# Batch 1's first half computed second, and the attention of the first two chunks in plain float32 with two heads side by side on the array

## The chip, the cores and the metric

The kernel runs on one core of a Trainium2 chip. The metric is the device time of one execution in microseconds. Names of engines in the profile: PE is TensorE's matmuls, PEld its weight loads, DVE is VectorE, ACT is ScalarE, POOL is GpSimd, SP is the queue from which all DMAs are issued.

## What is computed

Attention with a few sink positions and a sliding window, and behind it a two-layer MLP with a squared ReLU. Batch 4, 8 heads, 768 positions, head dimension 64; `n_sink` is 4 and `window` 128 at run time; the MLP has width 512 and inner width 2048.

```python
scores = (1 / sqrt(64)) * q @ k.T
keep = (k_pos < n_sink) | ((0 <= q_pos - k_pos) & (q_pos - k_pos < window))
a = exp(where(keep, scores, -1e9) - max); a = a / (a.sum(-1) + 1e-9)
x = (a @ v) as (batch * seq, heads * 64)
h = x @ w_in; out = (s * relu(h)**2 + b) @ w_out
```

## The kernel before

The work is cut into eight chunks of 384 positions, a half of a batch each, in the order of batches and halves. A chunk is attended by eight heads in blocks of 128 queries, and then goes through the MoE function (`moe_steps`, L513): for each of 16 tiles of the inner width, `l1` (L524: 12 matmuls of 384 columns, then ReLU, square, and a split into a high and a low part) and, two tiles later, `l2` (L543: 9 matmuls of 512 columns). While chunk c is in its MoE, the attention of chunk c+1 is interleaved with it, slot by slot (L691 to L703).

Products are made with two numbers each in a fast format, a rounded high part and the remainder (tiles of type float32r), except in the first chunk. For chunks 1 to 7 (`attn_slots`, L389) q, k, v and the turned probabilities are split so (L268 to L279, L321, L322), scores are two matmuls of up to 272 columns (L293, L294), and sums of the sink positions and the reciprocals go through a matrix of their own (L305 to L386). A second half has four key blocks, a first half three. Chunk 0 (`first_slots`, L419) has nothing to hide behind and is computed in plain float32: q is held twice, with zeros for the other head of its pair (L429, L430), and for each head and block there is one score product over all 128 partitions (L446), mask and maximum (L448), exponential (L452), after a head's three blocks the scaling by its reciprocal sum (L460 to L463), transposes (L471) with a copy (L475), and the product with v of both heads, of which one half of the partitions is kept (L483 to L486).

The 16 weight tiles come as raw 64-bit words and are made into float32 pairs during chunk 0's attention and MoE (`make_weight`, L189): two conversions on ScalarE (L198, L199), two bit operations on VectorE (L200, L201), an addition on GpSimd (L203), a rounding copy on ScalarE (L208) and the remainder (L214), on GpSimd for one tile in four, else on VectorE. Raw words wait in the place of the next tile; those of the last tile lie in two `g` buffers (L178), of which `l1` has three.

The program is written in slots and steps, but a planner puts each engine's queue in an order by the readiness that it computes, and gives out buffers; only marked instructions keep the program's order.

## Time and profile before

| | us |
|---|---|
| median of three runs (lowest, highest) | 776.92 (775.92, 777.3) |
| the profiled execution | 775.58 |
| its span, first to last instruction | 773.6 |
| TensorE busy (matmuls) | 733.7, 95% |
| VectorE busy | 514.3, 66% |
| ScalarE busy | 501.5, 65% |
| GpSimd busy | 269.6, 35% |

The busy shares are means over stretches that differ. A stretch is read in the table of windows, an instruction's price in the groups by line, an order and a wait in the timelines. A matmul's end is modelled, so the distance between starts tells more than a duration.

### The profile page before, as it was taken

The page shows a single profiled execution, that of the slowest core. Times are in us where ns is not written, and L with a number is a line of the kernel's source. Part 1 is how long each engine was busy: PE and PEld are TensorE (multiplying, and loading weights), DVE is VectorE, ACT ScalarE, POOL GpSimd, SP SyncE. Part 2 cuts the span into 40 slices and gives each one's busy share as a digit, 9 for nine tenths or more (in the row PEclk, how much of TensorE's full clock was granted, in tenths as well). Part 3 has the DMA queues.
Part 4 walks back from the last instruction along what each step waited for, and adds up shares of the span by engine and source line. Part 5 has one row for each costly group of instructions (what it writes and reads, how often), then busy time and mean ns, then how long its engine had stood idle before and what let it go on. Part 6 is the DMA issues. An engine that isn't in the chain of part 4 may idle for free.

```text
span 773.6 us, 12079 instructions
## 1 busy us (share of the span) xinstructions
PE 733.7 (95%) x3980; PEld 652.9 (84%) x3980; DVE 514.3 (66%) x1251; ACT 501.5 (65%) x1231; POOL 269.6 (35%) x439
## 2 busy tenths in 40 slices
PE   6888887799999999999999999999999999999996
PEld 3567675589989999999989999999999999899985
DVE  5988998985676566765676566765676566763221
ACT  3996977776676577666676576766676576653222
POOL 3147567652333234332334234332334234310000
PEclk8998998889999999999999999999999999999999
DMA  8644304212111211112111211112112211001001
GB/s 271 277 146 182 112 14 162 86 34 76 44 44 53 86 47 54 50 44 77 43 44 55 85 47 54 50 43 77 43 43 57 84 47 54 29 1 42 0 1 46
DMA packets 28117, 54.21 MB, mean 70 GB/s; under 512 B 3600, under 2 KB 16528, under 8 KB 26128
## 3 DMA queue, kind: packets, MB, share of 16 engines
q1 hardware_dynamic: 28048, 53.36, 21.4%
q8 instruction: 34, 0.56, 0.3%
q14 instruction: 35, 0.29, 0.1%
HBM read 47.06 MB, written 6.29 MB: 69 GB/s over the span
## 4 chain that ended last, share of the span: by engine, by line
PE 76%; DVE 8%; ACT 7%; POOL 3%; issue 2%; DMA 1%; SPq 1%; POOLq 0%; ACTq 0%; DVEq 0%
PE h L524 32%; PE po L543 29%; PE o L355 3%; PE sc L294 2%; PE sc L293 2%; PE tp L317 2%; POOL w L203 2%; PE tp L316 2%; DVE w L201 1%; DVE g L532 1%; ACT w L199 1%; PE os L381 1%; DMA sb<-in_s 1%; PE ts L370 1%; DVE wt L200 1%
## 5 line engine op out<-in xcount | busy, mean ns | idle before, releaser
L543 PE MATMUL po<-w,g 128*128 128x512 f32 x1152 | 304.2, 404 | 7.6 <-ACT g L531 4.2
L524 PE MATMUL h<-x,w 128*128 128x384 f32 x1536 | 302.6, 346 | 6.3 <-DVE r L529 1.9
L524 PEld LDWEIGHTS h<-x,w 128*128 128x128 f32 x1536 | 272.5, 192 | 13.2 <-DVE r L529 3.2
L543 PEld LDWEIGHTS po<-w,g 128*128 128x128 f32 x1152 | 210.2, 190 | 49.6 <-DVE g L532 5.6
L527 ACT ACTIVATE r<-h 128x384 f32<-128x384 f32 x128 | 62.8, 491 | 104.2 <-PE h L524 97.6
L298 DVE CUSTOM_DVE_ANT_0 sm<-sc,msk 128x272 f32<-128x272 f32 (+1 forms) x168 | 70.0, 417 | 73.6 <-PE sc L294 64.4
L532 DVE SCALAR_TENSOR_TENSOR g<-r,sb,g 128x384 fp32r<-128x384 f32 x128 | 88.0, 687 | 45.6 <-ACT g L531 43.5
L529 DVE SCALAR_TENSOR_TENSOR r<-h,sb,r 128x384 f32<-128x384 f32 x128 | 78.5, 613 | 50.7 <-ACT r L527 50.6
L305 POOL COPY psk<-sm 128x48 f32<-128x48 f32 x168 | 47.0, 280 | 166.4 <-ACT sm L304 165.7
L304 ACT ACTIVATE sm<-sm,negm 128x272 f32<-128x272 f32 (+1 forms) x168 | 85.2, 507 | 23.4 <-DVE negm L298 17.4
L531 ACT ACTIVATE g<-r,sb 128x384 fp32r<-128x384 f32 x128 | 78.7, 615 | 27.7 <-DVE r L529 25.9
L273 POOL TENSOR_TENSOR kl<-kraw,kh 128x544 fp32r<-128x544 f32 (+1 forms) x56 | 71.5, 1277 | 54.9 <-ACT kh L271 50.8
L321 ACT CAST hl<-tp 128x256 fp32r<-128x256 f32 (+1 forms) x168 | 59.0, 352 | 24.1 <-PE tp L317 23.6
L322 DVE TENSOR_TENSOR hl<-tp,hl 128x256 fp32r<-128x256 f32 (+1 forms) x168 | 66.6, 397 | 6.2 <-ACT hl L321 5.3
L278 POOL TENSOR_TENSOR vv<-vraw,vv 128x256 fp32r<-128x256 f32 (+1 forms) x56 | 40.8, 728 | 54.1 <-ACT vv L277 49.7
L364 DVE TENSOR_TENSOR xm<-o,y 64x512 f32<-64x512 f32 x56 | 38.5, 687 | 31.3 <-ACT y L363 18.9
L355 PE MATMUL o<-hl,vv 128*128 128x256 f32 (+1 forms) x288 | 54.5, 288 | 0.8 <-DVE r L529 0.7
L294 PE MATMUL sc<-kl,qs 128*128 128x272 f32 (+1 forms) x168 | 48.8, 291 | 0.3 <-POOL kl L273 0.3
L293 PE MATMUL sc<-kh,qs 128*128 128x272 f32 (+1 forms) x168 | 47.6, 283 | 1.4 <-DVE hl L322 1.4
L203 POOL TENSOR_TENSOR w<-w 128x1024 int32<-128x1024 int32 (+1 forms) x17 | 32.9, 1934 | 37.4 <-DVE z L461 19.4
L317 PE MATMUL tp<-identr,sm 128*128 128x128 f32 x168 | 45.9, 273 | 0.0
L272 DVE TENSOR_TENSOR qs<-qraw,qs 64x384 fp32r<-64x384 f32 x56 | 40.4, 721 | 6.9 <-ACT qs L268 5.3
(116 smaller groups left out, 895.5 us busy)
## 6 DMA issues: line engine op xcount, KB each, us to landing
w<-in_w SPq DMA_DIRECT2D x15, 1024.0 KB, 10.0
kraw<-in_kT SPq DMA_DIRECT2D x32, 272.0 KB, 2.6
out<-ot SPq DMA_DIRECT2D x24, 256.0 KB, 2.0
qraw<-in_qT SPq DMA_DIRECT2D x28, 192.0 KB, 2.4
kraw<-in_kT SPq DMA_DIRECT2D x24, 208.0 KB, 2.4
vraw<-in_v SPq DMA_DIRECT2D x16, 256.0 KB, 2.7
vraw<-in_v SPq DMA_DIRECT2D x12, 192.0 KB, 2.3
vsraw<-in_vsk SPq DMA_DIRECT2D x28, 64.0 KB, 1.8
```

The source lines that it names most:

```text
L273: nc.gpsimd.tensor_tensor(out=hd.kl[:, :kw], in0=hd.k[:, :kw], in1=hd.kh[:, :kw].bitcast(F32), op=ALU.subtract)
L293: nc.tensor.matmul(sc[:, :n], hd.qs[:, qs], hd.kh[:, c0:c0 + n], start=True, stop=False)
L294: nc.tensor.matmul(sc[:, :n], hd.qs[:, qs], hd.kl[:, c0:c0 + n], start=False, stop=True)
L298: nc.vector.tensor_tensor_reduce(out=sm[:, :n], in0=sc[:, :n], in1=m, scale=-0.125, scalar=BIG, op0=ALU.add, op1=ALU.min, accum_out=negm[: ...
L304: nc.scalar.activation(sm[:, :n], sm[:, :n], AF.Exp, bias=negm[:, uu], scale=-1.0, accum_out=pp.zz[:, i, hh:hh + 1])
L322: nc.vector.tensor_tensor(out=lo, in0=tp[:, a:z], in1=hi.bitcast(F32), op=ALU.subtract)
L355: nc.tensor.matmul(hd.o[:, q0:q0 + n * P], hd.vv[:, kb, :], hd.hl[:, t, c0 * P:(c0 + n) * P], start=(hd.n == 0), stop=(i == BLK - 1 and kb ...
L524: nc.tensor.matmul(h[:, :CH], weight[f][:, 0, wi, cc * P:(cc + 1) * P], x[xi][:, cc, :], start=(i == 0), stop=(i == 11))
L529: nc.vector.scalar_tensor_tensor(out=r, in0=h[:, :CH], scalar=sw_ap, in1=r, op0=ALU.mult, op1=ALU.mult)
L531: nc.scalar.activation(gg[:, 0, :], r, AF.Identity, bias=b_ap, scale=1.0)
L532: nc.vector.scalar_tensor_tensor(out=gg[:, 1, :], in0=r, scalar=b_ap, in1=gg[:, 0, :].bitcast(F32), op0=ALU.add, op1=ALU.subtract)
L543: nc.tensor.matmul(po[tb], gg[:, gi, tsl], weight[f][:, 1, wi, :], start=(f == 0 and i == 0), stop=(f == NF - 1 and i == 2))
```

## The change

The chunks run in the order (batch, half) = (0,0), (1,0), (0,1), (1,1), (2,0), (2,1), (3,0), (3,1). The first two are computed by a new class `Plain` in float32, without the split into parts; both are first halves. The two heads of a pair are worked on together: the score product of each reads its 64 partitions of q and k, the product with v writes its 64 partitions of one PSUM bank, the transposes of both heads fill a bank, and one copy on ScalarE takes 512 columns. VectorE scales, ScalarE copies. Chunk 1's plain attention stands beside chunk 0's MoE, uses tiles of the split form for its own, and loads q, k and v of a pair into one buffer each. q is loaded once and without zeros. The loads of `s` and `b` go out behind the first pair's q and k, and `sw_ap` (L685) keeps its program order. The remainder of the weights is made on GpSimd for every second tile. The raw words of the last tile lie in four pieces, in `vv`, `vv`, `xm` and `y`. The weights' making starts one slot pair earlier. The diff, without the body of `first_slots`, which goes:

```diff
--- before.py
+++ after.py
@@ -15,6 +15,7 @@
 
 P = 128
 B, H, S, D = 4, 8, 768, 64
+ORDER = ((0, 0), (1, 0), (0, 1), (1, 1), (2, 0), (2, 1), (3, 0), (3, 1))
 NS = 16
 BLK = 3
 CH = BLK * P
@@ -31,7 +32,8 @@
 WARM0 = 14
 NARROW, NEARLY = 2, 8
 RB, VB = 2, 2
-E0, LB0, LC0 = 8, 4, 6
+E0 = 8
+FN, FB, FC = (4, 2), (6, 6), (9, 10)
 LB, LC, LD, L2 = 2, 4, 1, 2
 
 
@@ -52,7 +54,7 @@
     first_cm = tc.tile_pool(name="first", bufs=1)
     first = first_cm.__enter__()
     late = []
-    m_all = first.tile([P, 6 * P], MDT, tag="m", name="m_all")
+    m_all = const.tile([P, 6 * P], MDT, tag="m", name="m_all")
     m_full = [m_all[:, a * P:(a + j + 1) * P] for j, a in ((0, 0), (1, 1), (2, 3))]
 
     identr = const.tile([P, P], F32R, tag="identr", name="identr")
@@ -90,7 +92,7 @@
     nc.sync.dma_start(lim[:, 0, :], n_sink.partition_broadcast(P))
     nc.sync.dma_start(lim[:, 1, :], window.partition_broadcast(P))
 
-    sc0 = wk.tile([P, 8, P], F32, tag="g", name="sc0", bufs=3)
+    sc0 = first.tile([P, 8, P], F32, tag="sc0", name="sc0")
     rel, rel1, low, upp, kix, snk, tmp, tm2 = (sc0[:, j, :] for j in range(8))
 
 
@@ -108,7 +110,7 @@
 
         limf = const.tile([P, 4], F32, tag="limf", name="limf")
         tc.keep_in_program_order(nc.vector.tensor_copy(limf[:, 0:2], lim[:, :, 0].bitcast(U32)))
-        nc.vector.tensor_copy(limf[:, 2:4], lim[:, :, 1])
+        tc.keep_in_program_order(nc.vector.tensor_copy(limf[:, 2:4], lim[:, :, 1]))
         nc.vector.scalar_tensor_tensor(out=nw, in0=limf[:, 2:4], scalar=4294967296.0, in1=limf[:, 0:2],
                                        op0=ALU.mult, op1=ALU.add)
         nc.vector.tensor_scalar(out=nw, in0=nw, scalar1=0.0, scalar2=1024.0, op0=ALU.max, op1=ALU.min)
@@ -174,9 +176,9 @@
                 raws[f] = [raw.rearrange("p c (f t) -> p c f t", t=2)]
         else:
             raws[f] = []
-            for c in range(2):
-                raw = wk.tile([P, DM, 2], I32, tag="g", name="wraw", bufs=3)
-                nc.sync.dma_start(raw.rearrange("p f t -> p (f t)"), w[f, :, c, :])
+            for j, tag in enumerate(("vv", "vv", "xm", "y")):
+                raw = wk.tile([P, DM // 2, 2], I32, tag=tag, name="wraw", bufs=2 if tag == "vv" else 1)
+                nc.sync.dma_start(raw.rearrange("p f t -> p (f t)"), w[f, :, j // 2, j % 2 * DM:(j % 2 + 1) * DM])
                 raws[f].append(raw)
 
     def scratch(f, j):
@@ -184,7 +186,15 @@
         if len(raws[f]) == 1:
             tag = f"w{NF - 2 + f % 2}"
             return (late[0] if late else first).tile([P, 2, DM], I32, tag=tag, name="wt", bufs=1)
-        return wk.tile([P, DM], I32, tag="ot", name="wt")
+        return wk.tile([P, DM], I32, tag="ot", name="wt")[:, :raws[f][j].shape[1]]
+
+    def piece(f, j, t):
+
+        n = len(raws[f])
+        if n == 1:
+            return weight[f][:, :, t, :]
+        a = DM * 2 // n
+        return weight[f][:, j * 2 // n, t, j * a % DM:j * a % DM + a]
 
     def make_weight(j):
 
@@ -204,14 +214,12 @@
         if j % 2 == 1:
             weight[f] = place(f).bitcast(F32R)
             for c, raw in enumerate(raws[f]):
-                d = weight[f][:, :, 0, :] if len(raws[f]) == 1 else weight[f][:, c, 0, :]
-                nc.scalar.copy(d, raw[..., 1].bitcast(F32))
+                nc.scalar.copy(piece(f, c, 0), raw[..., 1].bitcast(F32))
         f -= 1
         if j % 2 == 0 and f >= 0:
             for c, raw in enumerate(raws[f]):
-                d = weight[f] if len(raws[f]) == 1 else weight[f][:, c]
-                e = nc.gpsimd if f % 4 == 3 else nc.vector
-                e.tensor_tensor(out=d[..., 1, :], in0=raw[..., 1].bitcast(F32), in1=d[..., 0, :].bitcast(F32), op=ALU.subtract)
+                e = nc.gpsimd if f % 2 == 1 else nc.vector
+                e.tensor_tensor(out=piece(f, c, 1), in0=raw[..., 1].bitcast(F32), in1=piece(f, c, 0).bitcast(F32), op=ALU.subtract)
             raws.pop(f)
 
 
@@ -220,7 +228,7 @@
 
     def new_chunk(c):
         k = Chunk()
-        k.c, k.b, k.half = c, c // 2, c % 2
+        k.c, (k.b, k.half) = c, ORDER[c]
         k.x = [wk.tile([P, NCC, CH], F32R, tag=f"x{i}", name=f"x{i}_{c}") for i in range(2)]
         k.cc, k.xx, k.heads, k.pairs = {}, {}, {}, {}
         return k
@@ -416,98 +424,139 @@
         return k, [slot(t) for t in range(n + LC + LD)]
 
 
-    def first_slots():
...
+    class Plain:
+
+        def __init__(self, c):
+            self.c, (self.b, _) = c, ORDER[c]
+            self.groups = ((0, 1), (2,))
+            if c == 0:
+                self.q = wk.tile([P, NCC, CH], F32, tag="x0", name="q0")
+                self.k = wk.tile([P, NCC, CH], F32, tag="x1", name="k0")
+                self.v = first.tile([P, NCC, BLK, 2, D], F32, tag="v0", name="v0")
+            self.x = [wk.tile([P, NCC, CH], F32R, tag=f"x{i}", name=f"x{i}_{c}") for i in range(2)]
+            self.pairs = {}
+
+        def load_first(self, ps_):
+            nc.sync.dma_start(self.q[:, ps_, :], qT[0, ps_, :, :CH].rearrange("r e s -> e r s"))
+            nc.sync.dma_start(self.k[:, ps_, :], k0[0, :, ps_, :])
+
+        def load_values(self):
             for ps_ in (slice(0, 1), slice(1, NCC)):
+                nc.sync.dma_start(self.v[:, ps_].rearrange("p r n h d -> p r n (h d)"),
+                                  v[0, ps_, :, :BLK].rearrange("r p n h d -> p r n (h d)"))
+
+        def load(self, pr):
+            pp = Chunk()
+            self.pairs[pr] = pp
+            if self.c == 0:
+                pp.q, pp.k, pp.v = self.q[:, pr], self.k[:, pr], self.v[:, pr]
+                return
+            pp.q = wk.tile([P, CH], F32, tag="qraw", name="qf", bufs=1)
+            nc.sync.dma_start(pp.q, qT[self.b, pr, :, :CH])
+            pp.k = wk.tile([P, CH], F32, tag="kraw", name="kf", bufs=1)
+            nc.sync.dma_start(pp.k, k0[1, :, pr, :])
+            pp.v = wk.tile([P, BLK, 2, D], F32, tag="vraw", name="vf", bufs=1)
+            nc.sync.dma_start(pp.v, v[self.b, pr, :, :BLK])
+
+        def scores(self, pr, group):
+
+            pp = self.pairs[pr]
+            if group == 0:
+                pp.sm = [None] * 4
+                pp.z = (wk if self.c else first).tile([P, 2, BLK, 2], F32, tag="zr" if self.c else "z0", name="zf", bufs=2)
+            banks = {}
+            for i in self.groups[group]:
                 for hh in range(2):
                     hs = slice(hh * D, (hh + 1) * D)
...
+                    j = (i // 2, hh)
+                    if j not in banks:
+                        banks[j] = ps("sc")
+                    c0, n = (0, P, 0)[i], (i + 1) * P
+                    nc.tensor.matmul(banks[j][:, c0:c0 + n], pp.q[hs, i * P:(i + 1) * P], pp.k[hs, :n], start=True, stop=True)
+            for i in self.groups[group]:
+                c0, n = (0, P, 0)[i], (i + 1) * P
+                for hh in range(2):
+                    j = 2 * (i // 2) + hh
+                    if pp.sm[j] is None:
+                        if self.c:
+                            tag = ("kh", "kl", "qs")[self.turn % 3]
+                            self.turn += 1
+                            pp.sm[j] = wk.tile([P, CH], F32, tag=tag, name="smf")
+                        else:
+                            pp.sm[j] = first.tile([P, CH], F32, tag="sm0", name="sm0", bufs=E0)
+                    sm = pp.sm[j][:, c0:c0 + n]
+                    u = (self.c * H + 2 * pr + hh) * BLK + i
+                    uu = slice(u, u + 1)
+                    nc.vector.tensor_tensor_reduce(out=sm, in0=banks[(i // 2, hh)][:, c0:c0 + n], in1=m_full[i], scale=-0.125, scalar=BIG,
+                                                   op0=ALU.add, op1=ALU.min, accum_out=negm[:, uu])
+                    nc.scalar.activation(sm, sm, AF.Exp, bias=negm[:, uu], scale=-1.0, accum_out=pp.z[:, 0, i, hh:hh + 1])
+
+        def norm(self, pr):
+
+            pp = self.pairs[pr]
+            nc.vector.tensor_scalar(out=pp.z[:, 1], in0=pp.z[:, 0], scalar1=1e-9, scalar2=None, op0=ALU.add)
+            nc.vector.reciprocal(out=pp.z[:, 0], in_=pp.z[:, 1])
+            for i in range(BLK):
+                c0, n = (0, P, 0)[i], (i + 1) * P
+                for hh in range(2):
+                    sm = pp.sm[2 * (i // 2) + hh][:, c0:c0 + n]
+                    nc.vector.tensor_scalar(out=sm, in0=sm, scalar1=pp.z[:, 0, i, hh:hh + 1], scalar2=None, op0=ALU.mult)
+
+        def turned(self, pr, part):
+
+            pp = self.pairs[pr]
+            if part == 0:
+                pp.t = (wk if self.c else first).tile([P, 2, 2 * BLK, P], F32, tag="hl" if self.c else "tt0", name="tf", bufs=2)
+            tp = (ps if self.c else po_bank)("tp")
+            pos = (((0, 0), (2, 2)), ((1, 0), (1, 1)), ((2, 0), (2, 1)))[part]
+            for hh in range(2):
+                for j, (i, kb) in enumerate(pos):
+                    c0 = (0, P, 0)[i] + kb * P
+                    nc.tensor.transpose(tp[:, (2 * hh + j) * P:(2 * hh + j + 1) * P], pp.sm[2 * (i // 2) + hh][:, c0:c0 + P], ident)
+            out = pp.t[:, :, part:part + (6 if part == 0 else 3):(5 if part == 0 else 2)]
+            nc.scalar.copy(out, tp.rearrange("p (h k c) -> p h k c", h=2, c=P))
+
+        def values(self, pr):
+            pp = self.pairs.pop(pr)
+            o = ps("o")
             for kb in range(BLK):
...
+                for hh in range(2):
+                    a = (0, 3, 5)[kb]
+                    hs = slice(hh * D, (hh + 1) * D)
+                    nc.tensor.matmul(o[hs, kb * P:CH], pp.v[:, kb, hh], pp.t[:, hh, a:a + BLK - kb].rearrange("p k c -> p (k c)"),
+                                     start=(kb == 0), stop=(kb == BLK - 1))
+            nc.scalar.copy(self.x[0][:, pr, :], o[:, :CH])
+            nc.vector.tensor_tensor(out=self.x[1][:, pr, :], in0=o[:, :CH], in1=self.x[0][:, pr, :].bitcast(F32), op=ALU.subtract)
+
+    def po_bank(name):
+        return psO.tile([P, 512], F32, tag="po", name=name)
+
+    def plain_slots(c):
+        k = Plain(c)
+        k.turn = 0
+        todo = {}
+
+        def at(t, fn, *a):
+            todo.setdefault(max(t, 0), []).append((fn, a))
+
+        first_one = c == 0
+        for pr in range(H // 2):
+            t = 6 * pr
+            at(t - (0 if first_one else 6), k.load, pr)
+            for g in range(len(k.groups)):
+                at(t + 2 * g, k.scores, pr, g)
+            for part in range(3):
+                at(t + FB[first_one] + part, k.turned, pr, part)
+            at(t + FN[first_one], k.norm, pr)
+            at(t + FC[first_one], k.values, pr)
 
         def slot(t):
             def f():
...
+                for fn, a in todo.get(t, ()):
+                    fn(*a)
             return f
 
-        return k, [slot(t) for t in range(n + LC0)]
+        return k, [slot(t) for t in range(max(todo) + 1)]
 
 
     def moe_steps(x, store, wk, before=None, last=False):
@@ -637,7 +686,7 @@
 
     def store_at(c):
         def f(tb, ot):
-            r0 = c * CH + tb * P
+            r0 = (2 * ORDER[c][0] + ORDER[c][1]) * CH + tb * P
             nc.sync.dma_start(out[r0:r0 + P, :], ot)
         return f
 
@@ -675,16 +724,22 @@
         return nc.values_load(flag, min_val=0, max_val=P)
 
     NC_ = 2 * B
-    k, slots = first_slots()
+    k, slots = plain_slots(0)
+    k.load_first(slice(0, 1))
+    nc.sync.dma_start(sb[:, 0:1], s.partition_broadcast(P))
+    nc.sync.dma_start(sb[:, 1:2], b.partition_broadcast(P))
+    constants()
+    k.load_first(slice(1, NCC))
+    k.load_values()
     for i, f in enumerate(slots):
         f()
         if i == 10:
             weights(4, 0)
         if i == 18:
             constants2()
-            nc.vector.tensor_scalar(out=sw_ap, in0=sb[:, 0:1], scalar1=1.0 / WUP, scalar2=None, op0=ALU.mult)
-        if i >= 22 and i % 2 == 0:
-            weights(NEARLY - 1, (i - 20) // 2)
+            tc.keep_in_program_order(nc.vector.tensor_scalar(out=sw_ap, in0=sb[:, 0:1], scalar1=1.0 / WUP, scalar2=None, op0=ALU.mult))
+        if i >= 20 and i % 2 == 0:
+            weights(NEARLY - 1, (i - 18) // 2)
     first_cm.__exit__(None, None, None)
     late_cm = tc.tile_pool(name="late", bufs=1)
     late.append(late_cm.__enter__())
@@ -692,7 +747,7 @@
         steps = moe_steps(k.x, store_at(c), wk, before if c == 0 else None, c == NC_ - 1)
         slots = []
         if c + 1 < NC_:
-            k, slots = attn_slots(c + 1)
+            k, slots = plain_slots(1) if c == 0 else attn_slots(c + 1)
         i = 0
         for j, st in enumerate(steps):
             st()
@@ -726,7 +781,7 @@
 
     kT = np.ascontiguousarray(np.concatenate([kT, kT], axis=2))
 
-    k0 = np.ascontiguousarray(k[0, :, :CH].transpose(0, 2, 1).reshape(H // 2, P, CH).transpose(1, 0, 2))
+    k0 = np.ascontiguousarray(k[:2, :, :CH].transpose(0, 1, 3, 2).reshape(2, H // 2, P, CH).transpose(0, 2, 1, 3))
     vp = np.ascontiguousarray(v.reshape(B, H // 2, 2, S // P, P, D).transpose(0, 1, 4, 3, 2, 5))
 
     vsk = np.zeros((B, H // 2, P, P), v.dtype)
```

## Rows read from the trace of the kernel before

**Rows 1.** Busy time of the engines in three stretches: from and to (us from the span's start), its length, then for PE, PEld, DVE, ACT and POOL the busy us with the number of instructions, then granted TensorE clock, DMA share and GB/s.
```profile
8.00:49.00 41.00, 30.08 (x139) 21.44 (x139) 30.28 (x111) 33.70 (x93) 7.94 (x13) 0.92 0.61 234
49.00:178.00 129.00, 108.24 (x511) 88.91 (x510) 116.24 (x196) 99.87 (x201) 81.16 (x78) 0.89 0.33 111
178.00:263.00 85.00, 84.87 (x484) 78.04 (x483) 56.13 (x148) 56.71 (x152) 29.02 (x56) 1.00 0.19 56
```

**Rows 2.** Timeline of the SP queue: the output stores (start, us, queue, line, operation, operands, count). Each of the first three rows is the first store of a chunk; the last row merges six stores, those of the last two chunks, and ends with the last of them.
```profile
177.62 3.08 SPq L641 DMA_DIRECT2D out<-ot  x3
...
262.91 3.07 SPq L641 DMA_DIRECT2D out<-ot  x3
...
351.35 3.08 SPq L641 DMA_DIRECT2D out<-ot  x3
...
698.78 69.47 SPq L641 DMA_DIRECT2D out<-ot  x6
```

**Rows 3.** Timeline of the first 34 us, three rows of SP and VectorE (start, us, engine, line, operation, shapes, count, and in brackets the idle time before it and what ended it).
```profile
6.68 0.48 SPq L496 DMA_DIRECT2D sb<-in_s  x1
...
13.58 0.15 DVE L685 TENSOR_SCALAR sb<-sb 128x1 f32<-128x1 f32 x1 [3.76 <-DMA sb<-in_s]
...
21.52 0.88 DVE L463 TENSOR_SCALAR sm<-sm,z 128x128 f32<-128x128 f32 x3
```

**Rows 4.** Groups of instructions by line and shape from 8 to 49 us (busy us, mean ns of one, then idle time before them).
```profile
L452 ACT ACTIVATE sm<-sm,negm 128x384 f32<-128x384 f32 x8 | 4.9, 611 | 0.0
...
L448 DVE CUSTOM_DVE_ANT_0 sm<-sc,m_all 128x384 f32<-128x384 f32 x8 | 4.4, 549 | 0.6 <-PE sc L446 0.6
...
L486 DVE TENSOR_TENSOR x<-o,x 64x384 fp32r<-64x384 f32 x7 | 3.8, 548 | 1.3 <-ACT x L485 1.1
...
L475 ACT COPY tt<-tp 128x384 f32<-128x384 f32 x8 | 3.8, 471 | 0.1
...
L485 ACT CAST x<-o 64x384 fp32r<-64x384 f32 x7 | 3.3, 472 | 0.3
...
L452 ACT ACTIVATE sm<-sm,negm 128x128 f32<-128x128 f32 x8 | 3.2, 399 | 3.3 <-DVE negm L448 3.2
...
L448 DVE CUSTOM_DVE_ANT_0 sm<-sc,m_all 128x128 f32<-128x128 f32 x8 | 2.3, 284 | 0.5 <-PE sc L446 0.4
L475 ACT COPY tt<-tp 128x128 f32<-128x128 f32 x8 | 2.1, 266 | 1.7 <-PE tp L471 1.7
...
L200 DVE TENSOR_SCALAR wt<-w 128x1024 int32<-128x1024 int32 x2 | 1.4, 692 | 0.6 <-ACT w L199 0.6
L461 DVE RECIPROCAL z<-z 128x3 f32<-128x3 f32 x8 | 1.4, 172 | 0.2
```

**Rows 5.** Timeline of TensorE: float32 products and transposes of chunk 0 behind one another (start, us to the modelled end of the last, count of passes).
```profile
31.84 1.46 PE L483 MATMUL o<-tt,v 128*128 128x384 f32 x6
33.14 0.39 PE L446 MATMUL sc<-k,q 128*128 128x128 f32 x2
33.37 0.49 PE L471 MATMUL tp<-identr,sm 128*128 128x128 f32 x3
33.69 1.46 PE L446 MATMUL sc<-k,q 128*128 128x256 f32 x6
```

**Rows 6.** Groups by line from 49 to 178 us (busy us, mean ns of one).
```profile
L532 DVE SCALAR_TENSOR_TENSOR g<-r,sb,g 128x384 fp32r<-128x384 f32 x16 | 18.4, 1150 | 2.7 <-ACT g L531 2.5
...
L200 DVE TENSOR_SCALAR wt<-w 128x1024 int32<-128x1024 int32 (+1 forms) x15 | 13.7, 922 | 3.3 <-ACT w L199 1.8 <-PE o L483 1.5
L273 POOL TENSOR_TENSOR kl<-kraw,kh 128x544 fp32r<-128x544 f32 (+1 forms) x9 | 13.6, 1514 | 4.5 <-ACT kh L271 4.4
L214 DVE TENSOR_TENSOR w<-w,w 128x1024 fp32r<-128x1024 f32 (+1 forms) x12 | 13.2, 1108 | 1.8 <-ACT w L208 1.7
...
L304 ACT ACTIVATE sm<-sm,negm 128x272 f32<-128x272 f32 x24 | 12.4, 519 | 0.2 <-DVE negm L298 0.2
L272 DVE TENSOR_TENSOR qs<-qraw,qs 64x384 fp32r<-64x384 f32 x9 | 10.8, 1198 | 0.3
...
L214 POOL TENSOR_TENSOR w<-w,w 128x1024 fp32r<-128x1024 f32 x3 | 8.1, 2710 | 2.1 <-ACT w L208 2.1
...
L330 POOL COPY psk<-zh 128x6 f32<-128x6 f32 x4 | 1.0, 256 | 4.3 <-DVE zh L329 4.3
...
L259 ACT CAST vs<-vsraw 128x128 fp32r<-128x128 f32 x3 | 0.9, 292 | 2.1 <-PE os L381 2.1
...
L328 DVE RECIPROCAL zr<-zr 128x6 f32<-128x6 f32 x4 | 0.7, 182 | 0.0
```

**Rows 7.** The MoE's first matmul in the view of one line: shortest, median and longest duration in ns, first and last start.
```profile
L524 PE MATMUL h<-x,w x1536: 331/337/681, 49.0 to 760.7; 128*128 128x384 f32 x192
```

**Rows 8.** One piece of the chain of work that ended last (start, us, engine, tile and line, count).
```profile
699.51 6.35 PE h L524 x36
```

**Rows 9.** Timeline of VectorE: two of the sixteen subtractions of L532 in chunk 0.
```profile
125.58 2.33 DVE L532 SCALAR_TENSOR_TENSOR g<-r,sb,g 128x384 fp32r<-128x384 f32 x1
...
154.71 0.62 DVE L532 SCALAR_TENSOR_TENSOR g<-r,sb,g 128x384 fp32r<-128x384 f32 x1
```

**Rows 10.** The tile `wraw` (raw values of the last weight): its load and its last use (durations in ns, first and last start in us).
```profile
L179 SPq DMA_DIRECT2D wraw<-in_w x2: 383/404/424, 123.8 to 129.5; - x2
...
L214 POOL TENSOR_TENSOR w<-wraw,w x2: 1300/1308/1317, 162.1 to 165.5; 128x512 fp32r<-128x512 f32 x2
```

71 lines of the change are left out of this document (removed).

## The prediction

> **What bounds the kernel now.** I read the stage windows first [rows 1]. From 178 us on TensorE is busy for 84.87 of 85 us at granted clock 1.00, so there the time is TensorE work and nothing else. Before that it is not. From 49 to 178 us (chunk 0's MoE, the sixteen weight tiles being made, chunk 1's attention) VectorE is busy 116.24 of 129 us (0.90), ScalarE 99.87, GpSimd 81.16, at clock 0.89; the same MoE without attention takes the last chunk 69.5 us [rows 2]. From 8 to 49 us (chunk 0's attention and the first weights) ScalarE leads with 33.70 of 41 us. The stores [rows 2] give the rhythm: chunk 0 ends at 177.62, the next periods are 85.29 (beside it a first half, three key blocks) and 88.44 (a second half, four). The timeline of the start [rows 3] shows one plain hole: VectorE stands 3.76 us in front of the scaling of `sb` (L685), until the tiny load issued at 6.68, queued behind all of the chunk's q, k and v (2.3 MB by their shapes), has landed. Without it ScalarE is busy 33.70 of 37.2 us, 0.905.
>
> So I cost the change on three stretches: A (8 to 49), B (49 to 178) and the TensorE-bound rest.
>
> **The rest: the order of chunks.** Beside the MoEs of chunks 1 to 6 stand three first halves and three second halves now, and two and four afterwards: batch 1's first half has moved into B, batch 0's second half out of it. One period of 85.29 becomes one of 88.44: **+3.15 us** [rows 2]. Nothing else in these stages is touched.
>
> **A.** The loads of `s` and `b` go out behind the first pair's q and k only (384 KB), and L685 keeps its place in program order: the 3.76 us hole goes. What is late next is the first exponential chain itself, and the other pairs' q and k, which have some 10 us until a second pair can use them. ScalarE: the exponentials are the same 24 (three groups of eight from 4.9 to 3.2 us, 12.1 in all, [rows 4]); the copies of transposed blocks were 24 of 128 to 384 columns (266 to 471 ns, 8.8 us in three groups) and become 12 of 512, which by the step of about 0.1 us per 128 columns are 0.575 us each, 6.9 us; the eight 64-partition copies to x at 0.472 us become four of 128 partitions, 1.9 us instead of 3.8. That is 3.8 us less: 29.9. VectorE: eight subtractions into x at 0.548 become four (2.2 less), and eight adds and reciprocals of 0.17 us become four. At the same density of 0.905 the stretch is 29.9/0.905 = 33.0 us. A pair's chain is coarser than a head's: behind the last exponential stand a second head's three scalings (0.88, [rows 3]) and a longer copy, so I add 1.5. A is 34.5 instead of 41: **-6.5**. Two memsets of q go too, at nothing: they ran before the masks were there. The earlier weight step and the piecewise last raws move work between A and B and add none.
>
> TensorE in A is not the bound, but its price matters in B. A float32 product is two passes: the six passes over 384, 256 and 128 columns take 31.84 to 33.14 = 1.30 us, three transposes 33.37 to 33.69 = 0.32 [rows 5]. A head is thus 1.30 for scores, 0.64 for its six transposes and 1.30 for values, 3.24, and eight heads 25.9 us. In the new form the two heads of a pair lie on partition halves (scores) and column halves (values). Every matmul in the trace fills 128x128, so their cost must be bounded: if the halves run side by side, 5.2 + 5.1 + 5.2 = 15.5 us a chunk; if one after the other, 25.9. I take **15.5**, because the two heads alternate in the queue and write disjoint banks or partitions; both ends stay in the range. The Trainium skill, "TensorE: Matmul & The Clock Gate", Part 3 (packing small matmuls), says that matmuls on different row or column groups run concurrently; by that the lower end holds, and no run here shows it yet.
>
> **B.** Chunk 1's split attention leaves (groups that lie partly outside the stretch taken at a chunk's count): on VectorE eleven groups from L272 (8 of its 9, 9.6 us) to L328, 46.8 us in sum; on ScalarE nine from L304 to L259, 42.9; on GpSimd seven from L273 to L330, 39.7 [rows 6]. In its place comes the plain form: on VectorE the mask-and-maximum 10.1 (as many and as wide as chunk 0's, three groups from 4.4 to 2.3, [rows 4]), scalings 8 x 0.88 = 7.0, x 2.2, the small ones 1.4, sum 20.7; on ScalarE 12.1 + 6.9 + 1.9 = 20.9; on GpSimd nothing. The low parts of weights 1, 5, 9 and 13 move from VectorE (1.108 us each, 4.4) to GpSimd (2.71, 10.8). The scalings now run beside GpSimd, which stretches VectorE: L200, also one input and a scalar, takes 0.692 us in A and 0.922 in B [rows 4, 6]. On 7.0 us that is +2.3; the ends are 0 and 6.0 (L532's stretch, 0.62 at its shortest to a mean of 1.15, [rows 6, 9]). The sums for B:
> VectorE 116.2 - 46.8 + 20.7 - 4.4 + 2.3 = 88.0; ScalarE 99.9 - 42.9 + 20.9 = 77.9; GpSimd 81.2 - 39.7 + 10.8 = 52.3; TensorE at full clock 69.5 + 15.5 = 85.0 (now 69.5 + 19.0 = 88.5, 19.0 being 88.44 - 69.47).
>
> VectorE still leads, but TensorE is then 3% behind it, and three engines that are nearly level wait for each other more often. Now the leader is busy 0.90 of the stretch; I take 0.86, an estimate, with 0.90 and 0.80 as ends: 88.0/0.86 = 102.3 us (97.8 to 110). **-26.7 us.** In favour of the upper density: two of the three `g` tiles hold the last raw weight from 123.8 to beyond 165.5 us [rows 10], which the change lifts by putting them where only split attention works; I count it at nothing beyond that density. The new pair loads have one buffer each, and v of the next pair waits for the values of this one: on SP the weights' loads are queued beside it. A planner orders the queues by readiness and not by the program (L685, written behind slot 18, stands at 13.58 us, [rows 3]), so I put this at nothing; without that cover each of the three later pairs would hold the weight loads behind it for about a third of B's slots.
>
> **Sum.** 773.6 - 6.5 - 26.7 + 3.15 = 743.6 us of span. The profiled execution took 775.58, 2.0 above its span, and the median is 776.92, 1.3 above that: 743.6 + 2.0 + 1.3 = **746.9 us**.
>
> **Rivals.**
> *The halves run one after the other.* TensorE needs 69.5 + 25.9 = 95.4 in B and becomes its bound: 95.4/0.86 = 110.9, 8.6 more; in A the last pair's values cost 1.3 more. Time 746.9 + 9.9 = **756.8**. For it: every pair of passes in the trace runs in a row. Against: the operands don't overlap.
> *GpSimd holds VectorE.* One L532 took 2.33 us, another 0.62 [rows 9], with nothing but GpSimd's work to differ beside them. All GpSimd work left in B is in weight operations of 1.9 to 2.7 us. If the 24 scalings each lose 0.7 us to one, VectorE is at 104.8 - 2.3 = 102.5, over 0.86 = 119.2: 16.9 more, **763.8**. Against: GpSimd's share falls from 0.63 to about 0.51.
> *Each half-array pass drains the array (slower than before).* A full-array matmul of 384 columns lasts at least 331 ns from issue to end, while 36 of them follow each other in 6.35 us, 176 ns each [rows 7, 8]: 155 ns are hidden only by overlap. If passes on halves lose that overlap, a plain chunk's 96 of them cost 96 x 0.155 = 14.9 us more than the 25.9: 40.8. Then B is (69.5 + 40.8)/0.86 = 128.3 and A is bound by TensorE at 40.8/0.905 = 45.1: -0.7 + 4.1 + 3.15 = +6.5, **783.4**. With a loss of about 0.13 us a pass the sum is nought, so from there it decides; nothing in the trace shows such a loss, and between halves and the full array a chunk changes only 24 times (two groups of scores and one of values a pair, in and out). The Trainium skill, "TensorEngine Tiling (Array Packing)", Key Properties, says that a change of the tiling mode drains TensorE, a tile change within a mode doesn't: by that the loss is paid 24 times a chunk, not 96, an estimate of 3.7 us, and the forecast would be about 1 us later.
>
> **How the numbers follow.** Forecast 0.52, halves in a row 0.25, GpSimd holding VectorE 0.14, drains 0.05; 0.04 for a gain that is eaten otherwise. The range: from the upper density, A at 33 us and scalings unstretched (B 85.7/0.90 = 95.2: 738.3, and some for the freed `g`) to the GpSimd case: 734 to 766. A measurement of this kernel tells about 0.2% from no change. Slower by that: 0.05, the drain case; within it 0.03; faster 0.92 (the other cases).
>
> **What the new profile would show.** L685 without its wait and chunk 0's last float32 product near 42 us; in the stage behind it about 102 us to chunk 0's stores, VectorE and TensorE both high, GpSimd near 52 us; pairs of half matmuls starting together, and six passes of two heads in about 1.3 us and not 2.6; one more period of 88.4. Wrong it would be by passes of halves in a row, by scalings of over 1 us, by weights that arrive late (TensorE waiting for L208 or L214), or by periods after chunk 0 that differ from 85.3 and 88.4.

## The result and the profile after

The changed kernel takes **753.45 us** (median of four, 752.74 to 756.41) beside 776.42 (775.37 to 777.3): a ratio of 0.9712 [0.9682, 0.9742], 23.0 us less. The forecast was 746.9, in a range of 734 to 766. The profiled execution took 752.74, its span is 751.0.

Windows of the kernel after, whose rows answer to [rows 1] (columns: stretch, length, busy time and count of PE, PEld, DVE, ACT and POOL, granted TensorE clock, DMA share, GB/s):

```profile
8.00:45.00 37.00, 24.00 (x133) 13.84 (x133) 27.89 (x95) 29.90 (x73) 10.42 (x10) 0.79 0.70 281
45.00:151.00 106.00, 94.73 (x479) 75.66 (x478) 93.15 (x163) 79.95 (x155) 51.49 (x31) 0.93 0.29 106
151.00:240.00 89.00, 88.92 (x511) 81.65 (x510) 58.59 (x148) 59.47 (x154) 31.63 (x57) 1.00 0.23 67
```

Its output stores, in the timeline of the SP queue, answer to [rows 2]:

```profile
151.31 0.96 SPq L690 DMA_DIRECT2D out<-ot  x2
...
239.92 3.05 SPq L690 DMA_DIRECT2D out<-ot  x3
328.40 3.04 SPq L690 DMA_DIRECT2D out<-ot  x3
413.70 3.33 SPq L690 DMA_DIRECT2D out<-ot  x3
```

Two marks cut each trace into the three stretches of the forecast: the first matmul of the MoE (49.00 before, 44.97 after) and the first store (177.62 and 151.31). A is 4.0 us shorter (forecast 6.5), B 128.6 - 106.3 = 22.3 (forecast 26.7), and the rest, 596.0 before and 599.7 after, 3.7 longer (forecast 3.15). The stores show where most of the 3.7 lie: behind chunk 0 come periods of 88.61 and 88.48 before the first of 85.30, where there was one of 85.29 and then one of 88.44.

TensorE's timeline after (start, us to the modelled end, line, operands, count, idle time before it and what ended it): the values of one pair, two heads, and what follows them; ahead of them the first two pairs' scores.

```profile
6.41 1.57 PE L475 MATMUL sc<-k,q 64*128 64x128 f32 x12
11.14 1.88 PE L475 MATMUL sc<-k,q 64*128 64x128 f32 x12 [3.16 <-DMA k<-in_k]
...
25.12 1.51 PE L526 MATMUL o<-tf,v 128*64 128x384 f32 x12 [1.91 <-ACT tf L517]
26.57 0.92 PE L475 MATMUL sc<-k,q 64*128 64x128 f32 x6
```

Twelve passes on column halves take 26.57 - 25.12 = 1.45 us, two heads for little more than one head's 1.30 [rows 5]: the halves do run side by side. The second row is a surprise: TensorE, done with the first pair at 7.98, stands 3.16 us for the second pair's k, which the forecast had put well in time.

A second surprise is on VectorE. Its timeline, an undisturbed stretch and then the last pair of chunk 0:

```profile
26.31 0.17 DVE L497 TENSOR_SCALAR zf<-zf 128x6 f32<-128x6 f32 x1 [1.43 <-ACT sm L492]
...
26.74 1.67 DVE L503 TENSOR_SCALAR sm<-sm,zf 128x128 f32<-128x128 f32 x6
...
33.30 1.22 DVE L222 TENSOR_TENSOR w<-w,w 128x1024 fp32r<-128x1024 f32 x1
34.43 1.86 DVE L497 TENSOR_SCALAR zf<-zf 128x6 f32<-128x6 f32 x1
...
36.55 3.81 DVE L503 TENSOR_SCALAR sm<-sm,zf 128x128 f32<-128x128 f32 x6
```

and GpSimd's timeline beside the second:

```profile
33.51 2.75 POOL L213 TENSOR_TENSOR w<-w 128x1024 int32<-128x1024 int32 x1 [7.55 <-ACT tf L517]
37.50 2.65 POOL L222 TENSOR_TENSOR w<-w,w 128x1024 fp32r<-128x1024 f32 x1 [1.23 <-ACT w L217]
42.77 1.89 POOL L213 TENSOR_TENSOR w<-w 128x1024 int32<-128x1024 int32 x1 [2.62 <-DVE w L211]
```

An addition over six elements a partition takes 0.17 us at 26.31 and 1.86 at 34.43; there it ends at 36.29, when GpSimd's addition ends (36.26). Six scalings take 1.67 us free and 3.81 beside L222. Together 3.8 us on the chain that ends chunk 0's attention. GpSimd is held in its turn: its addition at 33.51 starts beside VectorE's subtraction L222 (33.30 to 34.52) and takes 2.75 us, the same one at 42.77 takes 1.89.

A third thing stands at the end of A. From 40 to 46 us the granted clock is 0.50, the lower of TensorE's two levels (1.2 GHz), behind TensorE's waits of 2.45 us for ScalarE's copies (to 33.02) and 1.93 us for the held scalings (to 40.42); in the kernel before it was 1.00 from 33 us to the end of A. The last pair's twelve passes on column halves take 44.97 - 42.21 = 2.76 us and not 1.45. TensorE's timeline there, the windows of the two places, and last the end of A in the kernel before:

```profile
42.21 2.83 PE L526 MATMUL o<-tf,v 128*64 128x384 f32 x12 [0.68 <-ACT tf L517]
...
25.00:26.60 1.60, 1.48 (x14) 0.81 (x14) 0.26 (x2) 1.60 (x6) 0.97 (x1) 1.00 1.03 415
42.00:45.00 3.00, 2.79 (x13) 1.26 (x13) 0.69 (x1) 2.27 (x3) 1.89 (x1) 0.50 0.00 0
...
33.00:49.00 16.00, 12.19 (x61) 8.20 (x59) 12.60 (x36) 15.68 (x40) 4.38 (x4) 1.00 0.02 5
```

VectorE's groups by line from 45 to 151 us answer to [rows 6] (busy us, mean ns of one, idle time before them):

```profile
L581 DVE SCALAR_TENSOR_TENSOR g<-r,sb,g 128x384 fp32r<-128x384 f32 x16 | 18.2, 1138 | 3.8 <-ACT g L580 3.7
...
L503 DVE TENSOR_SCALAR smf<-smf,zf 128x128 f32<-128x128 f32 (+2 forms) x24 | 10.9, 513 | 0.1
L578 DVE SCALAR_TENSOR_TENSOR r<-h,sb,r 128x384 f32<-128x384 f32 x16 | 9.8, 612 | 3.3 <-ACT r L576 3.2
...
L490 DVE CUSTOM_DVE_ANT_0 smf<-sc,m_all 128x128 f32<-128x128 f32 (+2 forms) x24 | 8.9, 414 | 0.0
L497 DVE TENSOR_SCALAR zf<-zf 128x6 f32<-128x6 f32 x4 | 3.0, 756 | 0.2 <-ACT smf L492 0.2
```

### The profile page after: what moved, and what is told of

Read it like the earlier page. It is cut to its first block, busy times and chain, and to the rows that moved or that the text cites. A ratio compares the mean times of both kernels' runs of the same rounds, so it can differ in the third digit from the quotient of the medians.

```text
span 751.0 us, 11834 instructions
## 1 busy us (share of the span) xinstructions
PE 718.3 (96%) x3976; PEld 635.6 (85%) x3976; DVE 490.6 (65%) x1205; ACT 481.0 (64%) x1169; POOL 244.5 (33%) x391
## 4 chain that ended last, share of the span: by engine, by line
PE 81%; DVE 8%; ACT 3%; DMA 3%; issue 2%; POOL 1%; SPq 1%; ACTq 0%; DVEq 0%; POOLq 0%
PE h L573 33%; PE po L592 32%; PE o L363 4%; PE sc L302 2%; PE sc L301 2%; PE tp L325 2%; PE tp L324 2%; DMA vf<-in_v 2%; DMA w<-in_w 2%; DVE g L581 1%; DVE wt L210 1%; DVE w L211 1%; POOL w L213 1%; PE os L389 1%; PE o L526 1%
## 5 line engine op out<-in xcount | busy, mean ns | idle before, releaser
L578 DVE SCALAR_TENSOR_TENSOR r<-h,sb,r 128x384 f32<-128x384 f32 x128 | 78.6, 614 | 53.8 <-ACT r L576 53.7
L306 DVE CUSTOM_DVE_ANT_0 sm<-sc,msk 128x272 f32<-128x272 f32 (+1 forms) x144 | 60.7, 422 | 65.7 <-PE sc L302 60.4
L580 ACT ACTIVATE g<-r,sb 128x384 fp32r<-128x384 f32 x128 | 78.9, 617 | 29.9 <-DVE r L578 29.0
L312 ACT ACTIVATE sm<-sm,negm 128x272 f32<-128x272 f32 (+1 forms) x144 | 73.8, 512 | 28.1 <-DVE negm L306 20.8
L313 POOL COPY psk<-sm 128x48 f32<-128x48 f32 x144 | 36.3, 252 | 154.7 <-ACT sm L312 154.1
L281 POOL TENSOR_TENSOR kl<-kraw,kh 128x544 fp32r<-128x544 f32 (+1 forms) x48 | 61.0, 1270 | 67.4 <-ACT kh L279 62.6
L329 ACT CAST hl<-tp 128x256 fp32r<-128x256 f32 (+1 forms) x144 | 51.3, 356 | 23.0 <-PE tp L325 22.4
L330 DVE TENSOR_TENSOR hl<-tp,hl 128x256 fp32r<-128x256 f32 (+1 forms) x144 | 57.9, 402 | 9.3 <-ACT hl L329 8.5
L286 POOL TENSOR_TENSOR vv<-vraw,vv 128x256 fp32r<-128x256 f32 (+1 forms) x48 | 33.2, 693 | 49.3 <-ACT vv L285 47.1
L213 POOL TENSOR_TENSOR w<-w 128x1024 int32<-128x1024 int32 (+1 forms) x17 | 32.6, 1920 | 45.4 <-DVE w L211 24.9
L363 PE MATMUL o<-hl,vv 128*128 128x256 f32 (+1 forms) x256 | 47.4, 287 | 0.0
L302 PE MATMUL sc<-kl,qs 128*128 128x272 f32 (+1 forms) x144 | 41.4, 287 | 0.0
L279 ACT CAST kh<-kraw 128x544 fp32r<-128x544 f32 (+1 forms) x48 | 29.0, 604 | 13.9 <-PE sc L301 8.7
```

The lines of the kernel that those rows point to most:

```text
L281: nc.gpsimd.tensor_tensor(out=hd.kl[:, :kw], in0=hd.k[:, :kw], in1=hd.kh[:, :kw].bitcast(F32), op=ALU.subtract)
L302: nc.tensor.matmul(sc[:, :n], hd.qs[:, qs], hd.kl[:, c0:c0 + n], start=False, stop=True)
L306: nc.vector.tensor_tensor_reduce(out=sm[:, :n], in0=sc[:, :n], in1=m, scale=-0.125, scalar=BIG, op0=ALU.add, op1=ALU.min, accum_out=negm[: ...
L312: nc.scalar.activation(sm[:, :n], sm[:, :n], AF.Exp, bias=negm[:, uu], scale=-1.0, accum_out=pp.zz[:, i, hh:hh + 1])
L330: nc.vector.tensor_tensor(out=lo, in0=tp[:, a:z], in1=hi.bitcast(F32), op=ALU.subtract)
L363: nc.tensor.matmul(hd.o[:, q0:q0 + n * P], hd.vv[:, kb, :], hd.hl[:, t, c0 * P:(c0 + n) * P], start=(hd.n == 0), stop=(i == BLK - 1 and kb ...
```

## The experiments

All runs, cut at the two marks of their own traces (us of the profiled execution; median, and ratio with its 95% interval to runs of the kernel before on the same chip, whose medians were 775.69 to 776.61). The profiled execution of e10_noadd took 736.36, more than its median, so its row shows rather too much:

| kernel | A ends | B | rest | median | ratio |
|---|---|---|---|---|---|
| before | 49.00 | 128.6 | 596.0 | 776.42 | 1 |
| after | 44.97 | 106.3 | 599.7 | 753.45 | 0.9712 [0.9682, 0.9742] |
| e1_row | 46.87 | 108.4 | 599.3 | 756.83 | 0.9761 [0.9747, 0.9775] |
| e2_split | 45.20 | 125.2 | 599.5 | 771.28 | 0.9939 [0.9924, 0.9953] |
| e3_quarter | 44.05 | 104.8 | 599.9 | 750.87 | 0.9685 [0.9672, 0.9698] |
| e4_g | 44.90 | 106.9 | 600.7 | 754.37 | 0.9745 [0.972, 0.977] |
| e5_order | 50.14 | 117.1 | 599.9 | 769.03 | 0.9909 [0.9887, 0.9931] |
| e6_sb | 49.24 | 127.2 | 596.5 | 775.46 | 0.9986 [0.9974, 0.9998] |
| e7_pair1 | 41.89 | 105.3 | 600.2 | 749.2 | 0.965 [0.963, 0.9669] |
| e8_all | 43.49 | 104.3 | 599.9 | 749.54 | 0.9669 [0.9644, 0.9693] |
| e10_noadd | 43.97 | 90.2 | 600.4 | 731.53 | 0.9423 [0.9403, 0.9444] |
| e11_q_p1 | 42.01 | 104.7 | 600.6 | 750.07 | 0.966 [0.9637, 0.9682] |
| e12_all_p1 | 40.39 | 104.4 | 599.9 | 746.72 | 0.9629 [0.9607, 0.9652] |
| e13_q_p1_act | 48.75 | 109.9 | 600.5 | 761.38 | 0.9812 [0.9792, 0.9832] |

The rest is 599.3 to 600.7 in every kernel with the new order and 596.0 to 596.5 in the two with the old one. So whatever an edit does shows in A and B.

My theory after the result: the gain has the parts that were forecast, and the missing 6.6 us are the second pair's late k and GpSimd's hold on VectorE. Its rivals: the order alone does more or less than it was priced at, and the loads of raw weights or passes on halves cost what was put at nothing.

**The order alone: e5_order**, on the kernel before.

```diff
+ORDER = ((0, 0), (1, 0), (0, 1), (1, 1), (2, 0), (2, 1), (3, 0), (3, 1))
...
-        k.c, k.b, k.half = c, c // 2, c % 2
+        k.c, (k.b, k.half) = c, ORDER[c]
...
-            r0 = c * CH + tb * P
+            r0 = (2 * ORDER[c][0] + ORDER[c][1]) * CH + tb * P
```

> Kernel before with nothing but the new order of chunks: batch 1's first half stands beside chunk 0's MoE by split attention, and one more second half beside the later MoEs. Theory: the later periods cost 3.15 us more, the stretch of chunk 0's MoE gets about as much shorter, since a first half has three key blocks; 775 to 778 us. Rival (the order itself is a gain, a lighter chunk where VectorE leads): 772 us or less.

The rival held: 769.03, 7.3 us less than the kernel before on the same chip (776.37). B is 11.5 us shorter, the rest 3.9 longer. Split attention of a first half, with three key blocks instead of four, is that much lighter in the stretch where VectorE is the busiest engine. The window of e5_order:

```profile
49.00:167.00 118.00, 98.02 (x487) 81.53 (x488) 110.29 (x196) 97.33 (x200) 88.67 (x79) 0.96 0.35 117
```

VectorE is busy 110.29 us where it was 116.24 [rows 1], and denser, 0.935. In the forecast the lighter chunk was inside the sum for B (all of a second half's split attention was taken out) and had no price of its own, so the order looked like a pure loss of 3.15.

**The plain form of chunk 1: e2_split**, the changed kernel with chunk 1 in the split form (raw weights in two pieces in the place of `g`, and the masks in the first pool, as before).

```diff
-            k, slots = plain_slots(1) if c == 0 else attn_slots(c + 1)
+            k, slots = attn_slots(c + 1)
```

> Kernel after, but chunk 1 by split attention again (the last weight's raw words back in g, the masks back in the pool of chunk 0, which the space asks for). Theory (the gain is the work that the plain form takes from VectorE, ScalarE and GpSimd beside chunk 0's MoE): the stretch is again about 125 us, 768 to 774 us. Rival (the gain comes from the start, the loads and where raw words lie): below 762 us.

As the theory had it: 771.28, B 18.9 us longer than after. Its window has VectorE at 113.14 of 125 us and GpSimd at 90.19:

```profile
45.00:170.00 125.00, 98.60 (x484) 80.69 (x481) 113.14 (x190) 96.17 (x199) 90.19 (x84) 0.96 0.32 111
```

Against e5_order, whose chunk 1 has the same form, the plain form is worth 117.1 - 106.3 = 10.8 us in B, against e2_split 18.9. The two differ in whether half or a quarter of the remainders are on GpSimd, among other things; that this is the 8 us between them was not tried alone.

**Where the raw pieces lie: e4_g** puts two of the four raw pieces of the last weight into `g`, as before.

```diff
-            for j, tag in enumerate(("vv", "vv", "xm", "y")):
+            for j, tag in enumerate(("g", "g", "xm", "y")):
```

> Kernel after, but two of the four pieces of the last weight's raw words in g buffers again, so that two of three are held from the load to the last remainder. Theory (place of the raw words matters little): 753 to 757 us. Rival (the free g buffers make a good part of the gain): 761 us or more.

754.37; its interval overlaps the one of after. The freed `g` is worth nothing that can be told.

**The alternation of the halves: e1_row** runs all passes of one head, then all of the other.

```diff
-            for i in self.groups[group]:
-                for hh in range(2):
+            for hh in range(2):
+                for i in self.groups[group]:
...
-            for kb in range(BLK):
-                for hh in range(2):
+            for hh in range(2):
+                for kb in range(BLK):
```

> Kernel after, but with the loop over the two heads outside, so that the passes of one half of the array stand behind each other and the two halves can overlap only where they meet; same products, same other work. Theory (VectorE leads in chunk 0's MoE stretch, TensorE second): a value product of a pair takes about 2.6 us at full clock in place of 1.45, a chunk about 10 us more of TensorE, of which VectorE's lead hides part: 757 to 763 us. Rival (the gain comes from halves side by side, TensorE sets the stretch): the whole 10 us in each of two chunks, 768 us or more.

756.83, 3.4 us over after: a little under the lower edge of what the theory expected. TensorE's timeline at the same place:

```profile
24.73 2.21 PE L526 MATMUL o<-tf,v 128*64 128x384 f32 x12 [1.90 <-ACT tf L517]
26.87 0.92 PE L475 MATMUL sc<-k,q 64*128 64x128 f32 x4
```

The same twelve passes take 2.14 us instead of 1.45, at a granted clock of 1.00 in both places, so the alternation is worth 0.69 us there. The 2.60 of the expectation did not come: by the widths in the single records, the second head's first pass starts at 25.43, 0.70 us behind the first head's, and from there the two heads run side by side, each head's own passes one behind the other. Whether the planner's queue or the engine brings them together so early is not shown. A and B lose 1.9 and 2.1 us.

**What GpSimd does to VectorE: e3_quarter, e8_all, e10_noadd.** The first leaves a quarter of the remainders on GpSimd instead of half, the second none. The third is e8_all with the addition of the low word left out: the weights lack their low bits, and GpSimd has 2.72 us of work left in B.

```diff
-                e = nc.gpsimd if f % 2 == 1 else nc.vector
+                e = nc.gpsimd if f % 4 == 3 else nc.vector   # e3_quarter
+                e = nc.vector                                # e8_all, e10_noadd
...
-                nc.gpsimd.tensor_tensor(out=hi, in0=hi, in1=lo, op=ALU.add)   # e10_noadd
```

> Kernel after, but only every fourth weight's remainder on GpSimd, as before. VectorE has four more subtractions (4.4 to 4.9 us), GpSimd 10.8 us less. Theory (GpSimd's work stretches VectorE's): the two cancel, 752 to 755 us, and VectorE's scalings are shorter. Rival (GpSimd costs VectorE nothing, VectorE leads): 757 to 758 us.

> Kernel after, but all weights' remainders on VectorE: eight subtractions (some 9 to 11 us) more on VectorE, 21.6 us less on GpSimd. Theory (GpSimd's work holds VectorE about as long as VectorE would need for it): 749 to 752 us. Rival (the quarter's gain had another cause, VectorE's own work counts in full): 755 us or more.

> As the kernel with all remainders on VectorE, and GpSimd's addition of the low words (the last bits of the weights) is left out, so that GpSimd does nothing in chunk 0's attention and MoE but the masks and chunk 2's first head. Theory (GpSimd's additions stretch VectorE's scalings, remainders and bit operations): scalings of a pair take 1.67 us each time, L581 about 0.62 us, and the kernel takes 738 to 745 us. Rival (only the chain of a weight becomes shorter, VectorE's own sum stays): 747 us or more.

Giving VectorE, the forecast's bound of B, more to do does not cost the 4 to 11 us that it adds: 750.87, below even the theory's 752, and 749.54. That is 2.6 and 3.9 us under the kernel after; the intervals of the ratios still touch, so that this gain is small beside its noise, though every run of both lies below every run of after. And without GpSimd's addition it takes 731.53, more than the theory gave. The windows of B, e8_all first:

```profile
43.50:148.00 104.50, 95.54 (x481) 75.59 (x480) 92.33 (x174) 80.02 (x156) 34.70 (x21) 0.96 0.30 107
```

e10_noadd:

```profile
44.00:134.00 90.00, 89.89 (x480) 73.12 (x479) 77.39 (x174) 78.29 (x155) 2.72 (x2) 0.98 0.34 124
```

Both have 174 operations on VectorE, the same ones, and their busy time falls from 92.33 to 77.39 us: 15 us of its "busy" was time held by GpSimd. TensorE, busy 89.89 of 90, is then the bound, and its own time has fallen too, from 95.54 us at a granted clock of 0.96 to 89.89 at 0.98. The groups by line show who was held, e8_all first:

```profile
L222 DVE TENSOR_TENSOR w<-w,w 128x1024 fp32r<-128x1024 f32 (+1 forms) x15 | 23.1, 1550 | 0.1
...
L503 DVE TENSOR_SCALAR smf<-smf,zf 128x128 f32<-128x128 f32 (+2 forms) x24 | 10.1, 482 | 0.0
```

e10_noadd:

```profile
L221 DVE TENSOR_TENSOR w<-w,w 128x1024 fp32r<-128x1024 f32 (+1 forms) x15 | 16.1, 1079 | 0.0
...
L580 DVE SCALAR_TENSOR_TENSOR g<-r,sb,g 128x384 fp32r<-128x384 f32 x16 | 10.1, 630 | 3.7 <-ACT g L579 3.6
...
L502 DVE TENSOR_SCALAR smf<-smf,zf 128x128 f32<-128x128 f32 (+2 forms) x24 | 6.8, 348 | 0.0
```

The subtraction into `g` is 630 ns free and 1138 in the kernel after; the scalings 348 and 513. In e8_all, where GpSimd has the additions alone, the subtraction into `g` is at 642. What these times cost B shows in TensorE's waits there (what waits, for what, us in total, times, longest), the kernel after first, then e8_all:

```profile
PE tp L515 <- DVE smf L503: 7.7, 3, 2.9
...
PE tp L515 <- DVE smf L503: 5.8, 4, 3.5
PE h L573 <- DVE w L222: 2.9, 2, 1.5
```

In the kernel after TensorE stands 11.3 us in B, 7.7 of them for scalings, of which one at 90.75 took 2.53 us beside GpSimd's L222, where the median is 0.35. In e8_all it stands 9.0, in e10_noadd 0.1. So the 14 us of B are some 9 us of waits and 5.7 of TensorE's own time. Leaving the addition out also takes one step of some 2 us out of each weight's chain, so the waits are not all the hold; how they divide was not settled. In A e8_all frees the last pair in part: the addition over six elements still takes 1.86 us beside L213, but the scalings behind it are back at 1.67 (VectorE's timeline):

```profile
35.02 1.86 DVE L497 TENSOR_SCALAR zf<-zf 128x6 f32<-128x6 f32 x1
...
37.15 1.67 DVE L503 TENSOR_SCALAR sm<-sm,zf 128x128 f32<-128x128 f32 x6
```

**The start: e6_sb and e7_pair1.** e6_sb is the kernel before with the loads of `s` and `b` in front of all others. e7_pair1 is the changed kernel with the second pair's q and k loaded by themselves, and those of the last two pairs behind.

```diff
+                    nc.sync.dma_start(sb[:, 0:1], s.partition_broadcast(P))   # e6_sb
+                    nc.sync.dma_start(sb[:, 1:2], b.partition_broadcast(P))
                     load()
                     constants()
-                    nc.sync.dma_start(sb[:, 0:1], s.partition_broadcast(P))
-                    nc.sync.dma_start(sb[:, 1:2], b.partition_broadcast(P))
...
-    k.load_first(slice(1, NCC))                                                # e7_pair1
+    k.load_first(slice(1, 2))
+    k.load_first(slice(2, NCC))
```

> Kernel before with nothing but the loads of s and b in front of those of q, k and v. Theory: the wait of 3.76 us in front of L685 goes and chunk 0's attention ends that much earlier, since ScalarE and VectorE stand still meanwhile: 772 to 774 us. Rival (the next data are not there either, or the time is given back later): within 1.5 us of before.

> Kernel after, but the second pair's q and k are loaded by themselves in front of those of the last two pairs. Theory (the wait of 3.16 us for k of the second pair stands on the path, ScalarE has nothing else then): 750.5 to 752.5 us. Rival (the exponentials wait anyway, or the queue's two more loads delay the rest): 753 to 755 us.

The rival held: e6_sb gives 1.1 us and not the 3.76 of the hole, and nothing in A, which ends at 49.24. The two issues ahead of q and k cost up to 2 x 0.48 us [rows 3] of it; ScalarE's timeline there shows the larger part, what was late next, the first weight:

```profile
17.31 1.10 ACT L198 ACTIVATE w<-w 128x1024 int32<-128x1024 uint32 x1 [3.24 <-DMA w<-in_w]
```

e7_pair1 gives 4.3 us (749.2), slightly more than expected: A ends 3.1 us earlier, and TensorE's wait for the second pair is down from 3.16 to 1.15. The first pair's scores stand earlier too, at 5.85 instead of 6.41:

```profile
5.85 1.57 PE L475 MATMUL sc<-k,q 64*128 64x128 f32 x12
8.57 1.58 PE L475 MATMUL sc<-k,q 64*128 64x128 f32 x12 [1.15 <-DMA k<-in_k]
```

**Together: e11_q_p1, e12_all_p1, e13_q_p1_act.** e11 is e3 with e7, e12 is e8 with e7, and e13 is e11 with the scalings on ScalarE, out of GpSimd's reach.

```diff
-                    nc.vector.tensor_scalar(out=sm, in0=sm, scalar1=pp.z[:, 0, i, hh:hh + 1], scalar2=None, op0=ALU.mult)
+                    nc.scalar.mul(sm, sm, pp.z[:, 0, i, hh:hh + 1])
```

> Kernel after with both edits: the second pair's q and k loaded by themselves, and all remainders on VectorE. Theory (two separate places, so the gains of 4.3 and 3.9 us add): 744.5 to 747 us. Rival (both take the same slack of VectorE): 748 to 750 us.

> Kernel after with the second pair's q and k loaded by themselves, and every fourth remainder on GpSimd. Theory (gains of 4.3 and 2.6 us add): 746 to 748 us. Rival (the two don't add): 749 to 751 us.

> As the kernel with every fourth remainder on GpSimd and the second pair's early load, and the scalings of the plain form on ScalarE. Theory (ScalarE leads in chunk 0's attention and is second in the stretch behind it, so what VectorE is spared comes back on ScalarE): 748 to 754 us. Rival (scalings held beside GpSimd are what the path consists of, ScalarE isn't held): 744 us or less.

e12_all_p1 has the lowest median of the kernels that leave nothing out, 746.72, as the theory had it (its interval overlaps that of e7), with A shorter than in e7 and e8 and B as short as in e8. With a quarter on GpSimd (e11) the two gains don't add: A is as in e7 and B as in e3, but e7's own B was only 0.6 us longer, and the interval of the ratio overlaps those of both parts. e13 is far slower than either expectation, and its windows say why:

```profile
8.00:49.00 41.00, 28.29 (x139) 15.50 (x136) 18.07 (x74) 36.05 (x95) 5.02 (x8) 0.78 0.63 252
49.00:159.00 110.00, 98.08 (x479) 73.47 (x480) 88.03 (x146) 92.10 (x182) 44.52 (x27) 0.97 0.28 100
```

The hold is gone from the scalings, but ScalarE leads in A, and the 24 scalings bring it to 36.05 of 41 us; in B it becomes the leader too, 92.10 against VectorE's 88.03.

## Why the prediction was right, and where it was short

The direction and the three stretches were right; the span came 7.4 us over the forecast's 743.6: 2.5 in A, 4.4 in B, 0.5 in the rest.

**Halves side by side: right.** 1.45 us for two heads' values, and by e1_row the alternation is worth 3.4 us. A drain at every pass is excluded by the same 1.45. A price for each change between half and whole array is there, 0.09 us (last section), or 24 x 0.09 = 2.2 us a chunk, which the forecast's 15.5 us left out; whether any of it reaches the time is not shown. The Trainium skill, "TensorE: Matmul & The Clock Gate", Part 3, says that matmuls on different row or column groups run at the same time; the trace agrees for float32 in two passes, 1.45 against 2.60 us.

**The order: right in the rest, unseen in B.** +3.15 was forecast for the rest and 3.7 measured, but the same move makes chunk 1 lighter in B, by 11.5 us in e5_order; of the whole gain of 23.0 the order alone gives 7.3.

**A: two steps failed.** ScalarE's 29.9 us came out to the hundredth, 29.90, which is luck: four casts for chunk 1 (1.8 us in the kernel before, L259 to L277) have left the stretch too, and the forecast did not count them. The density did not come out: 29.90 of 37.0 is 0.81, not 0.905. The first step that failed is "the other pairs' q and k, which have some 10 us until a second pair can use them": TensorE is ready for the second pair at 7.98 us and gets its k at 11.14. e7_pair1 shows the price, 3.1 us in A. The hole at L685 went, as said (its scaling, now L740, stands at 18.1 us without a wait), but "the 3.76 us hole goes" was not worth 3.76: in e6_sb ScalarE waits 3.24 us for the first weight instead, and A ends no earlier. The forecast also had no term for the last pair's hold by GpSimd, 3.8 us on the chain, of which e8_all gets 1.5 back, nor for the lower clock at the end, 1.3 us in the last pair's values (2.76 instead of 1.45; 2.75 in e7_pair1, e8_all and e12_all_p1 too). With the early load and all remainders on VectorE, in e12_all_p1, A ends at 40.39, before the 42.5 that the forecast gave.

**B: VectorE's sum near, one term too small, and TensorE's waits left out.** VectorE's sum was 88.0 and is 93.15; at the forecast's density of 0.86 that would be 108.3 us. The density was 93.15/106 = 0.88 and gave 2 back. Of the 5.1 us the scalings are 1.6 (10.9 instead of 9.3) and the additions over six elements 2.3 (3.0 instead of four times 0.17), both held by GpSimd. That VectorE leads did not hold: TensorE's 85.0 at full clock are 94.73 us at a granted clock of 0.93, a little more than VectorE's 93.15, and neither fills the 106. TensorE waits 7.7 us for scalings there, and for none in e10_noadd. The forecast's density stood for all such waits without naming one, so that it came close is in part luck. ScalarE (79.95, forecast 77.9) and GpSimd (51.49, forecast 52.3) were near.

**The rivals.** "GpSimd holds VectorE" was the true one by mechanism and too dear by size: it had each scaling lose 0.7 us, and they lose 513 - 348 = 165 ns in the mean (two of the 24 take 1.73 and 2.53 us), but it counted scalings alone. The hold is spread over many VectorE operations with all operands in SBUF, and some of it was in the kernel before too (L532 at 1150 ns [rows 6], 630 where GpSimd is idle), inside the rows from which the forecast took its prices. Halves in a row, and a drain at each of the 96 passes, are excluded by the 1.45 us.

**What stays open.** How the waits that e10_noadd takes off B divide between the hold and a shorter chain per weight; why e2_split is 8 us longer in B than e5_order; and why e5_order's A ends 1.1 us later than before's with nothing changed in chunk 0 (its granted clock from 33 us on was 0.92, where before's was 1.00).
